# Splitting scores on chip from unit 8 on, and issuing later scores two steps sooner

## The chip, the core and the metric

The kernel runs on one core of one Trainium2 chip. The metric is the device time of one execution in microseconds (us). A core has five engines with a queue each: TensorE (PE, matmuls; its weight loads are listed apart as PEld), VectorE (DVE), ScalarE (ACT), GpSimd (POOL) and SyncE (SP), which here only issues DMAs. Each engine takes its instructions in the order of its queue and waits on semaphores that other engines or DMAs raise.

## The reference

Two stages follow each other. The first is a gated linear recurrence over 4 batches, 8 heads and 768 positions, in chunks; the second a two-layer feed-forward with softplus over the 3072 tokens that come out.

```python
log_a = np.log(np.clip(a, 1e-06, 1.0))
for c in range(nc):                                   # chunks of 32
    cum = np.cumsum(la, axis=-1)
    L = np.exp(cum[:, :, :, None] - cum[:, :, None, :]) * causal
    M = np.einsum('bhin,bhjn->bhij', Cc, Bc) * L      # scores, weighed
    y_intra = np.einsum('bhij,bhjd->bhid', M, xc)
    y_inter = np.einsum('bhin,bhnd->bhid', Cc, state) * decay_to_i[:, :, :, None]
    y[:, :, sl] = y_intra + y_inter
    state = decay_full[:, :, None, None] * state + np.sum(Bx, axis=2)
...
h = x @ w_in                                          # 3072 x 256 @ 256 x 2048
g = np.maximum(h, 0.0) + np.log1p(np.exp(-np.abs(h)))
return (g @ w_out).astype(np.float32)                 # 2048 x 256
```

## The kernel before

**Units.** The recurrence is cut into 24 units of 128 positions, six for each batch; a unit holds all 8 heads. For unit i the names are: `un` its inputs (three buffers in turn), `rm` its decays, `sp_0` and `sp_1` the scores of heads 0-3 and 4-7 in two PSUM banks, `m` the weighed scores, `bp` and `cc` scaled B and C, `zp` the product that updates `state`, `tb` the state spread for reading, `yp_0`, `yp_1` the outputs in PSUM, `y` the grown output, and `xh`, `xl` its high and low part, which the feed-forward reads.

**Two ways to make scores.** The scores of a unit are C times B for 8 heads with 16 rows each, so operands must be laid out with zeros between heads. For units below `FIRST` (12) the host lays them out: `fst` holds, beside x, B and C, a block with the zeros in it, and the kernel multiplies in full fp32, 64 rows to each of the two matmuls (line 386). From unit `FIRST` on, `un` holds B and C stacked plain, 768 KB instead of 576 KB; `split_unit` makes a coarse and a fine row for each on chip: ACT and DVE each pass twice over 128x512 (lines 247 and 248, tiles `c_all` and `b_rows`), two DMAs put `c_all` into the one buffer `c_rows`, whose zeros stay, and four fp32r matmuls of 128x256 make the scores (line 391).

**Feed-forward.** Six token blocks j of 512, 16 feature tiles k each. A pair (j, k) is a first product into a PSUM bank `hp` (six matmuls of 128x512: line 563), softplus to `e` and its high part `gh` on ACT (lines 591, 597), the low part `gl` on DVE (line 603), and a second product of six matmuls into `acc` (line 642). The weights come as 64-bit floats, 512 KB at a time into `wraw`, and are taken apart on ACT and DVE into `wih`, `wil`, `woh`, `wol` (tile `w` on the way; weight step 12 gives `wih` and `wil` for k = 12 and 13). One PSUM pool of six banks serves `hp`, `sp`, `zp`, `yp`; a second holds `acc`.

**What sets the order.** Up to about 86 us the order is the string `ORDER`, written out by hand; everything issued in it stands under line 127 in the profile (the wrapper that keeps program order), and `U7` in it is a step of `update(7)`. After that a loop runs over steps s: `first` and the `e`, `gh`, `gl` of pair s, `second` of pair s-8, and the recurrence's work that `plan` put on step s. A scheduler then orders this part engine by engine. Units 8 to 11 have their scores at steps 20, 22, 25, 28 (`U_STEP`) and their values one step later. Units from 12 on have scores at step 4(i-4) and values two steps after. All DMAs are issued by SP, in program order.

Of the kernel before, what the change touches and what calls it, by code (L numbers as in the profile page):

```python
# [19 lines left out]
NB, NH, S, D, N = 4, 8, 768, 32, 16  # L20
SUB = 32
NC = P // SUB
NU = S // P
# [3 lines left out]
NFT = DFF // P  # L27
TOK = NB * S
HEAD = 4
FIRST = 12  # L30
GU = 3
U_X = 0
U_B = U_X + DM
# [17 lines left out]


ORDER = """
warm1 warm7 la kc hc0 kb un0 w0 loga hc1 loga un1 gb ft0 lr hc2 un2 fr0 ft0 S0 w2 fr0 hc3 D0 fr0 un3 gq0 un4
fr0 w1 D1 W0 gq2 M0 w4 gq0 fr2 M0 S1 gq2 D3 fr2 C1 I0 logr M1 ft2 logr B0 B1 growth U0 C2 U1 U0 W0 fr2
growth T1 B2 fr2 gd U1 ft2 U2 M1 un5 D2 U2 R1 W2 G0 S3 G0 C3 W0 S2 T3 M3 I1 warm3 T2 W0 w6 M2 W0 M3 R3 D4 M2
I3 G1 R2 S4 G1 X0 C4 W0 gg3 I2 warm2 X1 W4 B3 D5 M4 G2 H0 C5 M4 U3 H1 W2 G2 U3 W2 S5 warm4 X2 T4 W2 w3 G3 W2
B4 R4 un6 M5 G3 I4 W2 U4 D6 G4 W1 U4 H2 G4 M5 H3 X3 X4 F0.0 T5 W4 F0.1 W1 P0.0 W4 R5 P0.1 W1 F0.2 P0.0 W4 I5
P0.1 w5 W1 F0.3 W4 D7 w7 G5 S6 warm2 W1 un7 G5 gg6 P0.2 W4 X5 W6 F0.4 M6 P0.2 W6 M6 F0.5 P0.0 W1 P0.3 I6 W6
W3 Z0.0 B6 P0.3 W6 w8 P0.1 U6 W6 U6 C7 Z0.1 W3 W6 P0.4 G6 S7 W5 T7 W3 G6 P0.2 R7 P0.4 F0.6 X6 P0.5 M7 P0.5  # L60
W3 F0.7 w10 M7 W3 P0.3 I7 W3 P0.6 G7 W7 Z0.2 W5 G7 P0.4 X7 P0.7 Z0.3 W5 P0.6 P0.5 W5 P0.7 F1.0 w12 W7 W5
P0.6 F1.1 P1.0 W5 W7 W8 Z0.4 P0.7 P1.1 W7 P1.0 F1.2 w14 W8 B7 W7 W8 W7 Z0.5 P1.2 P1.0 W10 W8 F1.3 P1.1 w9
W10 W8 P1.1 Z0.6 W8 P1.3 W10 W14 F1.4 P1.2 W10 w11 P1.2 W10 Z0.7 W14 P1.4 W10 W14 W9 F1.5 P1.3 W9 W14 F1.6
P1.5 w13 P1.3 W14 W9 F1.7 P1.6 W14 W9 W11 F0.8 w15 W11 W9 W11 F0.9 W9 W11 W13 F0.10 K0 W13 W13 W11 F0.11 W13
W11 W13 Z1.0 W15 W13 W15 W12 U7 Z1.1 W15 P1.4 W12 P1.4 P1.5 Z1.2 W12 P1.7 P1.5 P1.6 W15 Z1.3 P0.9 P1.6 W15
W12 P1.7 Z1.4 U7 W15 P0.11 P1.7 W12 Z1.5 P0.9 W12 P0.10 P0.9 P0.11 Z1.6 P0.8 P0.11 P0.10 Z1.7 P0.10 P0.8 K1
P0.8 zero
"""
HALF = NFT // 2
AHEAD = 20  # L70
# [3 lines left out]
EARLY = 8  # L74
U_STEP = (20, 22, 25, 28)
# [29 lines left out]
def recurrence_then_ffn(ctx: ExitStack, tc: tile.TileContext, fst, un, at, al, w_in, w_out, const, outT):  # L105
# [28 lines left out]
    def load(out, in_):  # L134

        tc.keep_in_program_order(nc.sync.dma_start(out, in_))  # L136

    la = cp.tile([P, NB * NU * NH], F32, name="la")
    lr = cp.tile([P, S * NB * NH // P], F32, name="lr")
    cum = cp.tile([P, S * NB * NH // P], F32, name="cum")  # L140
    kc = cp.tile([P, K_END], F32, name="kc")
    kb = cp.tile([P, C_END], F32, name="kb")
# [6 lines left out]
    gd = dr.tile([NB, NH, S], F32, name="gd")  # L149
# [60 lines left out]
    def load_unit(i):  # L210
# [4 lines left out]
        un_s[i] = p3.tile([P, U_END], F32, tag="un", name=f"un{i}")  # L215
        if i < FIRST:
            load(un_s[i][:, :F_END], fst[i])
        else:
            load(un_s[i], un[i - FIRST])

# [17 lines left out]
    def split_unit(i):  # L238
        if i < FIRST:
            return  # L240
        t = un_s[i]
        b_rows = p2.tile([P, NQ, P], F32R, tag="b_rows", name=f"b_rows{i}")

        def split(out, j):
            raw = t[:, U_S + j * NQ * P : U_S + (j + 1) * NQ * P].rearrange("p (q t) -> p q t", q=NQ)
            g, be = (kb[:, C_GB + v : C_GB + v + 1] for v in (2 * j, 2 * j + 1))
            A.activation(out, raw, AF.Copy, scale=be)
            V.scalar_tensor_tensor(out, raw, g, out.bitcast(F32), op0=ALU.mult, op1=ALU.add)

        c_all = p2.tile([P, NQ, P], F32R, tag="c_all", name=f"c_all{i}")  # L250
        split(c_all, 1)
        for e in range(2):
            rows = slice(64 * e, 64 * e + 64)
            load(c_rows[rows, :, e].bitcast(F32), c_all[rows].bitcast(F32))
        split(b_rows, 0)
        st[i] = b_rows
# [121 lines left out]
    def score(i, g):  # L378
        sp = mid[i]["sp", g] = ps.tile([P, 512], F32, tag="ps", name=f"sp{i}_{g}")
        if i < FIRST:  # L380
            rows = slice(64 * g, 64 * g + 64)
# [292 lines left out]
    def prefetch(i):  # L674
        if i < NB * NU:
            load_unit(i)
            load_growth(i)
# [86 lines left out]
    def plan(s, f, *args):  # L764
        fills[s].append((f, args))

    for i in range(EARLY, NB * NU):
        s, wait = (U_STEP[i - EARLY], 1) if i - EARLY < len(U_STEP) else ((i - HEAD) * NFT // 4, 2)
        plan(s, prepare, i)
        plan(s, attend_scores, i)  # L770
        plan(s + wait, attend_values, i)
        if i + 2 < NB * NU:
            plan(s + 1, prefetch, i + 2)
    for i in range(EARLY, EARLY + 2):
        prefetch(i)
    for s in range(AHEAD, len(steps) + LAG):
        if s < len(steps):
# [56 lines left out]
```

## Time and profile before

| | |
|---|---|
| median of 3 runs (lowest to highest) | 341.74 us (340.98 to 342.81) |
| the profiled execution | 340.56 us, of which the span is 338.8 us |
| PE busy | 328.7 us, 97% of the span |
| DVE, ACT busy | 202.8 us (60%), 171.7 us (51%) |
| HBM read, written | 28.28 MB, 3.24 MB |

The span runs from the first instruction to the last; about 1.8 us of the execution lie around it. Busy times are of one engine; a group of instructions is named by its line, its engine and "output<-input". In the chain that ended last, each piece is followed back to what released it, so its shares add up to the span.

### The profile page before, as it was taken

How to read it: one execution, taken by the hardware profiler on the slowest of the kernel's cores; microseconds unless marked ns; L12 is line 12 of the kernel's file. 1: busy time of each engine (PE TensorE's matmuls, PEld its weight loads, DVE VectorE, ACT ScalarE, POOL GpSimd, SP SyncE). 2: the span in 40 equal slices, each digit the busy share in tenths (PEclk: the TensorE clock that was granted, in tenths of full speed). 3: DMA queues.
4: the chain of work that ended last, by engine and by line, in shares of the span. 5: the costliest groups of instructions: out<-in, count | busy, mean ns of one | idle time of the engine just before them, and what ended most of it. 6: DMA issues, size and time to landing. Idle time of an engine off the chain costs nothing.

```text
span 338.8 us, 5271 instructions
## 1 busy us (share of the span) xinstructions
PE 328.7 (97%) x2047; PEld 249.4 (74%) x2047; DVE 202.8 (60%) x394; ACT 171.7 (51%) x319; POOL 39.3 (12%) x32
## 2 busy tenths in 40 slices
PE   8789998999999999999999999999999999999995
PEld 4446657887666678778778778778778778888885
DVE  0899989996946444864765464777474342232242
ACT  4845666875715435445445455445445244444450
POOL 2434510000111010110112010111010000000000
PEclk9999999999999999999999999999999999999999
DMA  7964533573032205416434205443203100010001
GB/s 233 396 228 138 220 106 104 188 259 120 3 98 114 93 0 189 133 39 186 126 61 141 95 0 188 122 106 99 94 2 93 33 0 0 2 55 8 2 0 62
DMA packets 19376, 35.01 MB, mean 103 GB/s; under 512 B 1432, under 2 KB 10136, under 8 KB 19352
## 3 DMA queue, kind: packets, MB, share of 16 engines
q1 hardware_dynamic: 19352, 34.68, 31.5%
q8 instruction: 16, 0.26, 0.3%
q14 instruction: 8, 0.07, 0.1%
HBM read 28.28 MB, written 3.24 MB: 93 GB/s over the span
## 4 chain that ended last, share of the span: by engine, by line
PE 86%; DVE 6%; DMA 5%; SPq 1%; issue 1%; ACT 0%
PE hp L563 32%; PE acc L642 32%; PE hp L127 6%; PE acc L127 6%; PE yp L466 3%; DMA gg<-gd 3%; DMA head_in_l<-in_fst 2%; PE yp L450 2%; PE sp L391 2%; DVE m L127 1%; DVE w L127 1%; PE sp L386 1%; SPq L136 1%; PE zp L416 1%; PE end L127 1%
## 5 line engine op out<-in xcount | busy, mean ns | idle before, releaser
L603 DVE TENSOR_TENSOR gl<-e,gh 128x512 fp32r<-128x512 f32 x76 | 55.7, 734 | 61.3 <-ACT gh L597 61.1
L597 ACT CAST gh<-e 128x512 fp32r<-128x512 f32 x76 | 47.1, 620 | 61.1 <-PE acc L642 60.3
L591 ACT ACTIVATE e<-hp 128x512 f32<-128x512 f32 x76 | 45.1, 596 | 42.4 <-DVE gl L603 38.5
L563 PE MATMUL hp<-xh,wih 128*128 128x512 f32 x152 | 61.3, 405 | 0.0
L642 PE MATMUL acc<-gl,woh 128*128 128x512 f32 x155 | 60.6, 391 | 0.0
L642 PE MATMUL acc<-gh,wol 128*128 128x512 f32 x155 | 60.5, 391 | 0.0
L642 PE MATMUL acc<-gh,woh 128*128 128x512 f32 x155 | 59.6, 391 | 0.0
L563 PE MATMUL hp<-xl,wih 128*128 128x512 f32 x152 | 59.5, 392 | 0.0
L563 PE MATMUL hp<-xh,wil 128*128 128x512 f32 x152 | 59.3, 391 | 0.0
L345 POOL TENSOR_SCALAR_AFFINE_SELECT rm<-fc 128x1024 f32<-128x1024 f32 x16 | 23.8, 1487 | 187.7 <-DVE m L402 167.8
L563 PEld LDWEIGHTS hp<-xh,wih 128*128 128x128 f32 x152 | 28.5, 188 | 10.7 <-issue 3.1
L642 PEld LDWEIGHTS acc<-gh,woh 128*128 128x128 f32 x155 | 29.1, 188 | 6.8 <-issue 0.8
L642 PEld LDWEIGHTS acc<-gh,wol 128*128 128x128 f32 x155 | 29.1, 188 | 6.2
L642 PEld LDWEIGHTS acc<-gl,woh 128*128 128x128 f32 x155 | 29.1, 188 | 6.1 <-issue 0.2
L563 PEld LDWEIGHTS hp<-xh,wil 128*128 128x128 f32 x152 | 28.5, 188 | 6.3
L563 PEld LDWEIGHTS hp<-xl,wih 128*128 128x128 f32 x152 | 28.6, 188 | 5.1
L402 DVE TENSOR_TENSOR m<-sp,rm 128x512 f32<-128x512 f32 x32 | 20.9, 685 | 7.9 <-PE sp L391 6.3
L127 DVE SCALAR_TENSOR_TENSOR w<-wraw,w 128x512 int32<-128x512 int32 x32 | 23.1, 729 | 0.2
L127 PE MATMUL hp<-xh,wih 128*128 128x512 f32 (+1 forms) x48 | 17.7, 368 | 2.0 <-DVE m L127 1.4
L127 PE MATMUL hp<-xl,wih 128*128 128x512 f32 (+1 forms) x48 | 17.0, 354 | 0.0
L127 PE MATMUL hp<-xh,wil 128*128 128x512 f32 (+1 forms) x48 | 17.0, 354 | 0.0
L127 POOL TENSOR_SCALAR_AFFINE_SELECT rm<-fc 128x1024 f32<-128x1024 f32 x8 | 14.0, 1764 | 20.8 <-DVE m L127 15.0
(109 smaller groups left out, 409.6 us busy)
## 6 DMA issues: line engine op xcount, KB each, us to landing
un<-in_un SPq DMA_DIRECT2D x12, 768.0 KB, 4.4
un<-in_fst SPq DMA_DIRECT2D x8, 576.0 KB, 6.1
wraw<-in_w_in SPq DMA_DIRECT2D x8, 512.0 KB, 3.4
wraw<-in_w_out SPq DMA_DIRECT2D x8, 512.0 KB, 5.2
c_rows<-c_all SPq DMA_DIRECT2D x24, 128.0 KB, 2.4
out_t<-o SPq DMA_DIRECT2D x11, 256.0 KB
gg<-gd SPq DMA_DIRECT2D x14, 192.0 KB
head_in_l<-in_fst SPq DMA_DIRECT2D x4, 320.0 KB, 6.2
```

The costliest lines, as they stand in the source:

```text
L127: return lambda *a, **k: tc.keep_in_program_order(f(*a, **k))
L136: tc.keep_in_program_order(nc.sync.dma_start(out, in_))
L345: Pl.affine_select(out=rm.rearrange("p h c i -> p (h c) i"), in_=fc[:, u].rearrange("p h c -> p (h c)").unsqueeze(2).broadcast_to([P, NH * ...
L391: PE.matmul(sp[:, 2 * v * P : 2 * (v + 1) * P], b_rows[:, q], c_rows[:, q].rearrange("p e t -> p (e t)"), start=True, stop=True,)
L402: V.tensor_tensor(mid[i]["m"][:, 4 * g : 4 * g + 4].rearrange("p h t -> p (h t)"), mid[i].pop(("sp", g)), mid[i]["rm"][:, 4 * g : 4 * g + ...
L450: PE.matmul(yp[q // 2][out], tb[rows].rearrange("p e d -> p (e d)"), cc[rows].rearrange("p c i -> p (c i)"), start=True, stop=False,)
L466: PE.matmul(yp[g][32 * hh : 32 * hh + 32], un_s[i][:, U_X + h * D : U_X + (h + 1) * D], m[:, h, :], start=u == 0, stop=True,)
L563: PE.matmul(h[:, c0:c1], w[:, c, fs], x[:, c, c0:c1], start=i == 0, stop=i == 5)
L591: A.activation(e, h, AF.Softplus)
L597: A.copy(gh, e)
L603: V.tensor_tensor(gl, e, gh.bitcast(F32), op=ALU.subtract)
L642: PE.matmul(acc[:, c0:c1], wo[v, k // HK][:, k % HK, es], g[:, c0:c1], start=start and i == 0, stop=stop and i == 2,)
```

## The change

`FIRST` goes from 12 to 8, so units 8 to 11 are loaded, split and multiplied in the second way. The input of unit 10 is loaded ahead of the loop, with those of 8 and 9, and no longer at step 21. A step of `update(7)`, which reads the buffer that unit 10 takes over, is put earlier in `ORDER` (both `U7` move). From unit 12 on the scores move from step 4(i-4) to 4(i-4)-2, which is the step of the values of the unit in front, and stand behind them; the values stay at their step (wait 4 instead of 2), and the load of unit i+2 moves two steps forward with the scores.

```diff
-FIRST = 12
+FIRST = 8
...
-P1.2 W10 w11 P1.2 W10 Z0.7 W14 P1.4 W10 W14 W9 F1.5 P1.3 W9 W14 F1.6
+P1.2 W10 w11 P1.2 W10 Z0.7 W14 P1.4 W10 W14 W9 U7 F1.5 P1.3 W9 W14 F1.6
...
     for i in range(EARLY, NB * NU):
-        s, wait = (U_STEP[i - EARLY], 1) if i - EARLY < len(U_STEP) else ((i - HEAD) * NFT // 4, 2)
+        s, wait = (U_STEP[i - EARLY], 1) if i - EARLY < len(U_STEP) else ((i - HEAD) * NFT // 4 - 2, 4)
         plan(s, prepare, i)
         plan(s, attend_scores, i)
         plan(s + wait, attend_values, i)
-        if i + 2 < NB * NU:
+        if EARLY + 2 < i + 2 < NB * NU:
             plan(s + 1, prefetch, i + 2)
-    for i in range(EARLY, EARLY + 2):
+    for i in range(EARLY, EARLY + 3):
         prefetch(i)
```

(The lines of `ORDER` are wrapped differently after the change; only `U7` moves in them.) One line fewer stands in `ORDER`, so every line number below it is one lower after the change.

On PE, the scores of unit 8 stand where the hand-written order ends. `acc_1` is the second product of block 1, `hp_12` and `hp_13` first products of block 0. Before:

```order
L127 MATMUL acc_1_944<-gh_7_1003,woh_80 128x512
L563 MATMUL hp_12_1069<-xh_272,wih 128x512
L563 MATMUL hp_12_1069<-xl_273,wih 128x512
L386 MATMUL sp_0_1084<-un_1062 128x512
L386 MATMUL sp_1_1088<-un_1062 128x512
L563 MATMUL hp_13_1095<-xh_272,wih 128x512
```

After:

```order
L126 MATMUL acc_1_951<-gh_7_1005,woh_80 128x512
L562 MATMUL hp_12_1071<-xh_272,wih 128x512
L562 MATMUL hp_12_1071<-xl_273,wih 128x512
L390 MATMUL sp_0_1094<-c_rows,b_rows_1084 128x256 x2
L390 MATMUL sp_1_1099<-c_rows,b_rows_1084 128x256 x2
L562 MATMUL hp_13_1107<-xh_272,wih 128x512
```

The two full-fp32 matmuls give way to four fp32r ones at the same place.

On DVE, the stretch ahead of these matmuls. `un_1138` before and `un_1069` after are the inputs of unit 10, `un_1064` those of unit 9, `w_956` and `w_963` weight step 12, whose next reader is the ACT copy to `wih` for `hp_12`. Before:

```order
L127 TENSOR_TENSOR gl_4_973<-e_4_851,gh_4_970 128x512
L127 SCALAR_TENSOR_TENSOR w_956<-wraw_742,w_956 128x512
L127 TENSOR_TENSOR gl_5_986<-e_5_877,gh_5_975 128x512
L127 SCALAR_TENSOR_TENSOR w_952<-wraw_905,w_952 128x512
L360 TENSOR_TENSOR bp_1258<-un_1138,ft_127 128x128
L376 TENSOR_TENSOR cc_1260<-un_1138,fr_151 128x128
L127 TENSOR_TENSOR gl_6_999<-e_6_892,gh_6_988 128x512
L127 SCALAR_TENSOR_TENSOR w_956<-wraw_742,w_956 128x512
```

After:

```order
L126 TENSOR_TENSOR gl_4_975<-e_4_851,gh_4_972 128x512
L247 SCALAR_TENSOR_TENSOR c_all_1164<-un_1064,kb,c_all_1164 128x512
L247 SCALAR_TENSOR_TENSOR b_rows_1163<-un_1064,kb,b_rows_1163 128x512
L126 SCALAR_TENSOR_TENSOR w_963<-wraw_742,w_963 128x512
L126 TENSOR_TENSOR gl_5_988<-e_5_882,gh_5_977 128x512
L126 SCALAR_TENSOR_TENSOR w_959<-wraw_912,w_959 128x512
L359 TENSOR_TENSOR bp_1288<-un_1069,ft_127 128x128
L375 TENSOR_TENSOR cc_1290<-un_1069,fr_151 128x128
L126 TENSOR_TENSOR gl_6_1001<-e_6_899,gh_6_990 128x512
L247 SCALAR_TENSOR_TENSOR c_all_1270<-un_1069,kb,c_all_1270 128x512
L126 SCALAR_TENSOR_TENSOR w_963<-wraw_742,w_963 128x512
```

Three of the new split instructions are seen here; the two of unit 8 stand a little ahead of the first row, so five in all have come in front of the last one.

On PE, the values of unit 13 and what follows them. Before:

```order
L416 MATMUL zp_1661<-un_1403,bp_1612 32x64 x4
L450 MATMUL yp_0_1668<-cc_1614,tb_1659 64x128 x2
L450 MATMUL yp_1_1669<-cc_1614,tb_1659 64x128 x2
L466 MATMUL yp_0_1668<-m_1606,un_1403 32x128 x4
L466 MATMUL yp_1_1669<-m_1606,un_1403 32x128 x4
L563 MATMUL hp_7_1687<-xh_1134,wih 128x512
```

After:

```order
L449 MATMUL yp_1_1709<-cc_1616,tb_1699 64x128 x2
L465 MATMUL yp_0_1708<-m_1608,un_1443 32x128 x4
L465 MATMUL yp_1_1709<-m_1608,un_1443 32x128 x4
L390 MATMUL sp_0_1737<-c_rows,b_rows_1727 128x256 x2
L641 MATMUL acc_1_1525<-gh_15_1494,woh_855 128x512
L641 MATMUL acc_1_1525<-gl_15_1496,woh_855 128x512
L641 MATMUL acc_1_1525<-gh_15_1494,wol_856 128x512
L641 MATMUL acc_1_1526<-gh_15_1494,woh_855 128x512
L641 MATMUL acc_1_1526<-gl_15_1496,woh_855 128x512
L390 MATMUL sp_1_1742<-c_rows,b_rows_1727 128x256 x2
L641 MATMUL acc_1_1526<-gh_15_1494,wol_856 128x512
L562 MATMUL hp_7_1750<-xh_1146,wih 128x512
```

The scores of unit 14 now follow the values of unit 13 at once, and the next first product comes behind them.

More of the change, by code (lines that the diff above doesn't have):

```diff
@@ L53 @@
 ORDER = """
[L54 to L67, printed above, removed]
+warm1 warm7 la kc hc0 kb un0 w0 loga hc1 loga un1 gb ft0 lr hc2 un2 fr0 ft0 S0 w2 fr0 hc3 D0 fr0 un3 gq0 un4 fr0
+w1 D1 W0 gq2 M0 w4 gq0 fr2 M0 S1 gq2 D3 fr2 C1 I0 logr M1 ft2 logr B0 B1 growth U0 C2 U1 U0 W0 fr2 growth T1 B2
@@ new lines @@
+fr2 gd U1 ft2 U2 M1 un5 D2 U2 R1 W2 G0 S3 G0 C3 W0 S2 T3 M3 I1 warm3 T2 W0 w6 M2 W0 M3 R3 D4 M2 I3 G1 R2 S4 G1
+X0 C4 W0 gg3 I2 warm2 X1 W4 B3 D5 M4 G2 H0 C5 M4 U3 H1 W2 G2 U3 W2 S5 warm4 X2 T4 W2 w3 G3 W2 B4 R4 un6 M5 G3 I4
+W2 U4 D6 G4 W1 U4 H2 G4 M5 H3 X3 X4 F0.0 T5 W4 F0.1 W1 P0.0 W4 R5 P0.1 W1 F0.2 P0.0 W4 I5 P0.1 w5 W1 F0.3 W4 D7
+w7 G5 S6 warm2 W1 un7 G5 gg6 P0.2 W4 X5 W6 F0.4 M6 P0.2 W6 M6 F0.5 P0.0 W1 P0.3 I6 W6 W3 Z0.0 B6 P0.3 W6 w8 P0.1
+U6 W6 U6 C7 Z0.1 W3 W6 P0.4 G6 S7 W5 T7 W3 G6 P0.2 R7 P0.4 F0.6 X6 P0.5 M7 P0.5 W3 F0.7 w10 M7 W3 P0.3 I7 W3
@@ new lines @@
+P0.6 G7 W7 Z0.2 W5 G7 P0.4 X7 P0.7 Z0.3 W5 P0.6 P0.5 W5 P0.7 F1.0 w12 W7 W5 P0.6 F1.1 P1.0 W5 W7 W8 Z0.4 P0.7
+P1.1 W7 P1.0 F1.2 w14 W8 B7 W7 W8 W7 Z0.5 P1.2 P1.0 W10 W8 F1.3 P1.1 w9 W10 W8 P1.1 Z0.6 W8 P1.3 W10 W14 F1.4
+P1.2 W10 w11 P1.2 W10 Z0.7 W14 P1.4 W10 W14 W9 U7 F1.5 P1.3 W9 W14 F1.6 P1.5 w13 P1.3 W14 W9 F1.7 U7 P1.6 W14 W9
+W11 F0.8 w15 W11 W9 W11 F0.9 W9 W11 W13 F0.10 K0 W13 W13 W11 F0.11 W13 W11 W13 Z1.0 W15 W13 W15 W12 Z1.1 W15
+P1.4 W12 P1.4 P1.5 Z1.2 W12 P1.7 P1.5 P1.6 W15 Z1.3 P0.9 P1.6 W15 W12 P1.7 Z1.4 W15 P0.11 P1.7 W12 Z1.5 P0.9 W12
@@ L68 @@
+P0.10 P0.9 P0.11 Z1.6 P0.8 P0.11 P0.10 Z1.7 P0.10 P0.8 K1 P0.8 zero
 """
```

## The prediction, made before the changed kernel was run

> **What bounds the kernel now.** I read the page first, then the list of who waited for whom on PE, then busy time by stage, then the timeline of single engines around 75 to 93 us. The page:
>
> ```profile
> span 338.8 us, 5271 instructions
> PE 328.7 (97%) x2047; PEld 249.4 (74%) x2047; DVE 202.8 (60%) x394; ACT 171.7 (51%) x319; POOL 39.3 (12%) x32
> PE 86%; DVE 6%; DMA 5%; SPq 1%; issue 1%; ACT 0%
> ```
>
> 86% of the chain that ended last is PE itself. Where PE does wait (columns: engine and line, what it waited for, us in total, times, longest), the first and the last of nine rows:
>
> ```profile
> PE hp L127 <- DVE m L127: 1.4, 1, 1.4
> ...
> PE yp L127 <- ACT ft L127: 0.2, 1, 0.2
> ```
>
> They add up to 6.2 us, and all stand under line 127: none is in the scheduled loop. By stage (width, then busy time of PE, PEld, DVE, ACT, POOL with counts, clock, DMA share, GB/s):
>
> ```profile
> 54.00:86.00 32.00, 32.00 (x149) 26.09 (x148) 28.69 (x56) 23.17 (x41) 0.00 (x0) 1.00 0.51 166
> 86.00:134.00 48.00, 48.00 (x296) 33.17 (x295) 27.05 (x54) 22.09 (x40) 5.13 (x4) 1.00 0.26 88
> 134.00:283.00 149.00, 149.00 (x959) 117.28 (x958) 88.32 (x168) 72.00 (x128) 15.44 (x10) 1.00 0.29 86
> ```
>
> From 54 to 283 us PE is never idle and the granted clock is full. So in the whole stretch that the change touches, time goes only if PE gets less to do, and comes only if PE is made to wait. DVE is 90% busy just before (28.69 of 32.00) and 56% after.
>
> **Term 1: cheaper scores.** The two kinds of scores side by side: unit 8 before, and unit 12, which already goes the other way (start, us, line, forms, count):
>
> ```profile
> 86.35 0.39 PE L563 MATMUL hp<-xh,wih 128*128 128x512 f32 x1
> 86.58 0.39 PE L563 MATMUL hp<-xl,wih 128*128 128x512 f32 x1
> 86.90 1.13 PE L386 MATMUL sp<-un 64*128 64x512 f32 x4
> 87.96 0.50 PE L563 MATMUL hp<-xh,wih 128*128 128x512 f32 x1
> 88.29 0.39 PE L563 MATMUL hp<-xl,wih 128*128 128x512 f32 x1
> ...
> 133.61 0.39 PE L642 MATMUL acc<-gh,wol 128*128 128x512 f32 x1
> 133.84 0.64 PE L391 MATMUL sp<-c_rows,b_rows 128*128 128x256 f32 x4
> 134.31 0.40 PE L563 MATMUL hp<-xh,wih 128*128 128x512 f32 x1
> ```
>
> Durations overlap, so I count from start to start. A plain 128x512 matmul takes 0.23 (86.35 to 86.58). With full-fp32 scores it is 1.71 from 86.58 to 88.29 for two plain steps and the scores: 1.71 - 0.45 = 1.26 us, of which 1.06 are the scores and some 0.2 the slow step into them (0.32) and out of them (0.33). With fp32r it is 0.70 - 0.23 = 0.47, and no slow step. Each unit saves 0.79, four units 3.16 us, all on PE. Bounds: both forms are in the trace, so no more than 0.1 either way.
>
> A page bears on this price. The Trainium skill, "FP8 and Floating Point Precision", section Matmul Precision, says that true FP32 takes four passes through the array. My estimate by that page, with the passes of both matmuls one behind the other, would be 8 x 0.23 = 1.84 us for the scores instead of 1.06, and a saving of 6.3 us in all. The row shows 1.06 for both, the 64-row halves running together, so the row decides and the sum does not use the page.
>
> **Term 2: how the full-fp32 groups fall.** The remaining full-fp32 matmuls (zp, yp) also cost a slow step in and out wherever they are put among the others. Counting such groups without the scores in the instruction order, there are 35 before and 36 after: some units' zp and yp come together, others' yp is cut in two. A cut costs 0.09 in, 0.10 out (above) and the end of the last matmul; the shortest group in the trace bounds it:
>
> ```profile
> 108.07 0.39 PE L642 MATMUL acc<-gh,woh 128*128 128x512 f32 x1
> 108.38 0.32 PE L416 MATMUL zp<-un,bp 128*32 128x64 f32 x8
> 108.63 0.50 PE L642 MATMUL acc<-gl,woh 128*128 128x512 f32 x1
> 108.97 0.39 PE L642 MATMUL acc<-gh,wol 128*128 128x512 f32 x1
> ```
>
> 0.90 - 0.45 = 0.45 with its work, so between 0.2 and 0.45; I take +0.3.
>
> **Term 3: a new wait ahead of unit 8.** The splits of units 8 to 10 are now put into the queues of ACT and DVE between 75 and 92 us. DVE there, before (brackets: idle before it, and what ended it), and two splits of unit 12 for their pitch:
>
> ```profile
> 75.63 0.29 DVE L360 TENSOR_TENSOR bp<-un,ft 128x128 f32<-128x128 f32 x1
> 77.03 0.29 DVE L360 TENSOR_TENSOR bp<-un,ft 128x128 f32<-128x128 f32 x1 [0.31 <-DMA un<-in_fst]
> ...
> 83.71 0.29 DVE L360 TENSOR_TENSOR bp<-un,ft 128x128 f32<-128x128 f32 x1 [2.26 <-DMA un<-in_fst]
> 84.12 0.68 DVE L127 TENSOR_TENSOR gl<-e,gh 128x512 fp32r<-128x512 f32 x1
> 84.72 0.68 DVE L127 SCALAR_TENSOR_TENSOR w<-wraw,w 128x512 int32<-128x512 int32 x1
> ...
> 104.49 0.75 DVE L248 SCALAR_TENSOR_TENSOR c_all<-un,kb,c_all 128x512 fp32r<-128x512 f32 x1 [0.46 <-ACT c_all L247]
> 105.16 0.75 DVE L248 SCALAR_TENSOR_TENSOR b_rows<-un,kb,b_rows 128x512 fp32r<-128x512 f32 x1
> ```
>
> Five splits (c_all and b_rows of 8 and 9, c_all of 10) come in front of the `w` at 84.72: 5 x 0.67 = 3.35 us. They fill the idle 0.31 + 2.26 = 2.57, if the inputs of unit 10 are there when DVE asks. That `w` gives `wih` for `hp_12` through ACT:
>
> ```profile
> 80.86 0.62 ACT L127 CAST gh<-e 128x512 fp32r<-128x512 f32 x1 [0.25 <-PE acc L127]
> ...
> 84.83 0.60 ACT L127 ACTIVATE e<-hp 128x512 f32<-128x512 f32 x1 [1.82 <-DVE gl L127]
> 85.44 0.62 ACT L127 CAST wih<-w 128x512 fp32r<-128x512 f32 x1
> ```
>
> `wih` is done at 86.06 and `hp_12` starts at 86.35, so there is 0.29 of slack. The wait is 3.35 - 2.57 - 0.29 = 0.5 us. Behind `hp_12` PE holds everything, so this adds to the time one for one, once; later DVE has 44% idle to catch up. It can't be below 0, since PE has no idle to lose there. The high bound comes from the loads:
>
> ```profile
> 71.07 0.93 SPq L136 DMA_DIRECT2D un<-in_fst  x2
> 72.05 1.12 SPq L136 DMA_DIRECT2D gg<-gd  x2
> 77.94 0.33 SPq L136 DMA_DIRECT2D un<-in_fst  x1
> 134.51 1.27 SPq L136 DMA_DIRECT2D c_rows<-c_all  x2
> ...
> un<-in_un SPq DMA_DIRECT2D x12, 768.0 KB, 4.4
> c_rows<-c_all SPq DMA_DIRECT2D x24, 128.0 KB, 2.4
> ```
>
> The first two blocks, 1.18 MB, went out from 71.07 and had landed by 77.03, where DVE's wait for the second ends: 0.20 MB per us, or 0.33 if the 2.4 us that even a 128 KB copy takes are first set aside. Unit 8's block is 0.2 MB larger and so some 0.6 later; DVE took it at 75.63 without a wait, so 0.6 is the most that this adds. Unit 10's load goes out right behind `gg`, at about 73.2 instead of 77.94, since `U7` is out of its way. Three blocks and `gg` are 2.75 MB: landed by 71.1 + 2.4 + 8.3 = 81.8 at the second rate, 85.0 at the first. I take 81.8, because the fixed part is not paid for each. DVE asks for it at about 83.8; on ACT, c_all, e, woh, gh, e and wih, 0.6 each (84.83 to 85.44), must be done in a row, so ACT asks near 86.35 - 3.6 = 82.7. At the worst rate the wait is 0.5 + 85.0 - 82.7 = 2.8. I take 0.5, the sum of rows.
>
> **What I cost at nothing.** `U7` moved: the same zp on PE, and two DVE instructions of 0.3 at most (as `bp` above) between weights, ahead of 75 us. The copies to `c_rows` for unit 8: c_all is done some 2 us after 75.63, 1.27 for two issues and 2.4 to land end by 82, five us before PE asks. Those for unit 9 wait for unit 8's scores, done near 87.7: plus 1.27 and 2.4 is 91.4, while PE comes to them 25 plain steps, four score steps and one zp-yp group (about 1.5) after `hp_12` begins: 86.85 + 5.7 + 0.5 + 1.5 = 94.5. They now stand in SP's queue ahead of the load of unit 11, which waits for unit 8's yp (near 92.7) in any case; it lands 4.4 later at 97.1, and unit 9's second `m`, which stands behind unit 11's `cc` and a `gl` on DVE, is done 1.4 after that, at 98.5. PE needs it near 99.8 (16 plain steps, scores and most of a zp-yp group further). Had that load the 5.8 of unit 10's (77.94 to 83.71), it would be just in time. The splits of units 9 to 11 behind that are 1.3 us a unit on DVE and on ACT, under PE. Scores two steps sooner for units 12 to 23: PE does the same matmuls and waited for none of them, so nothing is to be had; DVE, ACT and SP merely change order.
>
> **Sum.** -3.16 + 0.3 + 0.5 = -2.4 us. The profiled execution took 340.56 (338.8 and 1.8 around it), 1.2 below the median shown, so it would become 338.2; against the median, 341.74 - 2.4 = 339.4 us, 0.7% less.
>
> **Rivals.** (a) The early wait eats the gain. For it: DVE is 90% busy up to 86 us, and one late load holds up everything behind it. The row at 83.71 shows that: `gl` at 84.12 had its input since `gh` ended near 81.5 and stood behind `bp`. The Trainium skill, "TensorE: Matmul & The Clock Gate", in its section on the array's architecture, says that ACT and DVE queues are strict FIFO; the trace agrees. If ACT's c_all of unit 10 is held by the load, every us past 82.7 is a us of PE; at 1.2 of wait (landing at 83.4) the change is under 0.5% (1.7 us, about what a measurement of this kernel can tell from no change), at 2.9 (85.1) it is nil: 341.7. Against it: 0.9 us between the landing I take and ACT's need. (b) The other side: PSUM banks. The scores of the next unit now come straight behind yp, so zp, two yp and two sp hold five of six banks when `hp` wants one, 0.24 + 1.13 + 0.24 + 0.23 = 1.84 us after yp ends. Had that to be the bank of the second `m`, free at about 2.5 (sp begins at 1.6, about 0.3 to its end, 0.6 for `m`, taken as a `gl`), PE would wait 0.65 on each of 12 units: 7.8 us, 347 us. It makes the kernel slower by 0.5% from 0.34 us a unit. Against it: zp's and yp's banks fall free earlier:
>
> ```profile
> 138.96 0.65 PE L466 MATMUL yp<-m,un 128*32 128x128 f32 x16
> 139.53 0.50 PE L563 MATMUL hp<-xh,wih 128*128 128x512 f32 x1
> ...
> 140.18 0.48 DVE L477 TENSOR_TENSOR y<-yp,gg 128x128 f32<-128x128 f32 x2
> ```
>
> `y` ends 1.1 us after yp here, 0.7 ahead of that. (c) Slightly more gain: no early wait and no cut, 338.6 or below.
>
> **How the numbers follow.** Forecast 0.58 (338.6 to 340.0), (c) 0.07, (a) 0.22 (340.0 to 343.4), (b) 0.13. Faster 0.65, same 0.22, slower 0.13. The range goes from 337.9, (c) with the scatter of a median, to 341.7, where (a) has eaten all; it leaves out (b) and the top of (a).
>
> **What would show it.** Four more units with line 390 matmuls 0.47 apart and no 64-row ones; a PE pause of about 0.5 before `hp_12` near 86.4, ended by ACT; no DVE wait for unit 10's load of 2 us; PE without idle from there to 283. It is wrong if PE waits again and again in the loop, or if unit 10 lands after 83.4.

## The result, and the profile after

The changed kernel is slower. Its median is 345.74 us (343.88 to 347.51, 4 runs) against 341.88 (340.98 to 342.81, 4 runs) for the kernel before on the same chip: ratio 1.0125, interval 1.0086 to 1.0164. The forecast was 339.4, the range 337.9 to 341.7. The profiled execution of the changed kernel took 345.08 us, 4.5 more than that of before. Ratios, here and below, are the record's over fast runs and not quotients of the medians; one run of e3 and one of e6 were slow and stand in those two medians alone.

The page after the change. The first row of engines answers to that of before; below it the clock that TensorE was granted, a digit for each fortieth of the span, and the chain that ended last by engine:

```profile
span 343.3 us, 5296 instructions
PE 330.2 (96%) x2047; PEld 251.6 (73%) x2047; DVE 208.7 (61%) x402; ACT 176.0 (51%) x327; POOL 38.6 (11%) x32
PEclk9899989999999999999999999999999999999999
PE 82%; DMA 7%; DVE 6%; ACT 2%; issue 1%; POOL 1%; SPq 1%; ACTq 0%; DVEq 0%; POOLq 0%
```

PE's share of the chain fell from 86% to 82% and that of DMA rose from 5% to 7%. The clock has two dips, in the second and sixth slice (9 to 17 and 43 to 51 us), both in the head; looked at closely they are two stretches at half clock, 14.42 to 17.83 and 48.55 to 51.96 us (granted clock 0.50 in each). By stage, in the same columns as in the prediction:

```profile
54.00:86.00 32.00, 32.00 (x151) 26.09 (x147) 30.57 (x61) 24.41 (x42) 0.00 (x0) 1.00 0.59 190
86.00:134.00 48.00, 44.99 (x292) 33.03 (x291) 34.38 (x63) 24.29 (x44) 7.79 (x5) 1.00 0.37 107
134.00:283.00 149.00, 149.00 (x953) 116.31 (x952) 84.89 (x165) 72.13 (x127) 12.00 (x9) 1.00 0.30 88
```

PE now stands still for 3.01 us of the 48 behind 86 us, where it had no idle before. PE's timeline there (in brackets the idle time ahead of a matmul, and what ended it):

```profile
87.80 0.39 PE L126 MATMUL acc<-gh,woh 128*128 128x512 f32 x1
90.06 0.50 PE L126 MATMUL acc<-gl,woh 128*128 128x512 f32 x1 [1.87 <-DVE gl L126]
...
91.94 0.51 PE L126 MATMUL acc<-gh,woh 128*128 128x512 f32 x1 [0.47 <-ACT gh L126]
92.95 0.50 PE L562 MATMUL hp<-xh,wih 128*128 128x512 f32 x1 [0.50 <-ACT wih L126]
93.29 0.40 PE L562 MATMUL hp<-xl,wih 128*128 128x512 f32 x1
93.52 0.63 PE L390 MATMUL sp<-c_rows,b_rows 128*128 128x256 f32 x4
93.99 0.40 PE L562 MATMUL hp<-xh,wih 128*128 128x512 f32 x1
```

From start to start, and less the 0.23 of a plain step, the three waits take 2.03, 0.62 and 0.78 us; a fourth at 86.54 takes 0.34. That is 3.8 us ahead of the scores of unit 8, where the prediction had 0.5. The scores themselves are as cheap as forecast: 0.70 from 93.29 to 93.99 for a plain step and the scores.

The chain of work that ended last, in order of time, tells whose wait it was (start, us, what):

```profile
80.77 0.69 SPq L135
...
81.50 8.05 DMA c_rows<-c_all
...
89.66 0.10 ACT c_all L246
...
90.29 0.58 ACT e L126
90.87 0.51 ACT woh L126
91.37 0.45 ACT gh L126
...
92.28 0.62 ACT wih L126
...
92.95 0.73 PE hp L562 x2
```

A copy of unit 8's `c_all` into `c_rows` took 8.05 us, where the median of these copies before was 2.4. What waits for it is not PE's scores but ACT, which wants to write the `c_all` of unit 10. Tiles `c_all` have two buffers, so unit 10 takes that of unit 8, and may do so only when the copies have read it. On ACT and DVE:

```profile
89.66 0.72 ACT L246 ACTIVATE c_all<-un,kb 128x512 fp32r<-128x512 f32 x1 [4.56 <-DMA c_rows<-c_all]
```
```profile
88.91 0.29 DVE L359 TENSOR_TENSOR bp<-un,ft 128x128 f32<-128x128 f32 x1 [1.82 <-DMA un<-in_un]
89.32 0.68 DVE L126 TENSOR_TENSOR gl<-e,gh 128x512 fp32r<-128x512 f32 x1
```

ACT stood for 4.56 us; `e`, `woh`, `gh` and `wih` queued behind. DVE stood for 1.82 for the load of unit 10, with the `gl` behind it that PE wanted at 88. Both transfers were late. SP's queue:

```profile
74.13 0.93 SPq L135 DMA_DIRECT2D un<-in_un  x2
75.11 1.26 SPq L135 DMA_DIRECT2D gg<-gd  x2
76.42 1.12 SPq L135 DMA_DIRECT2D un<-in_un  x1
80.77 14.70 SPq L135 DMA_DIRECT2D c_rows<-c_all  x4
```

The last row counts the copies of units 8 and 9 together; those of unit 8 are issued by 82.1.

The growth factors `gg` of unit 9 (two loads of 192 KB) go out just ahead of the load of unit 10. The load, issued from 76.42 on, is taken by DVE at 88.91: some 12 us later, where the one of 576 KB before took 5.8 (77.94 to 83.71). While all wait, the DMA engines are mostly idle (the last two columns are their busy share and GB/s):

```profile
78.00:84.00 6.00, 6.00 (x28) 4.95 (x27) 5.69 (x14) 5.35 (x10) 0.00 (x0) 1.00 1.03 313
84.00:90.00 6.00, 4.01 (x17) 2.67 (x15) 4.18 (x8) 1.44 (x3) 0.00 (x0) 1.00 0.23 72
```

A share of 0.23 and 72 GB/s, after 1.03 and 313 in the six us ahead: 0.23 of 16 is 3.7, so what is left would run on about four of the sixteen engines. The Trainium skill, "DMA: Bandwidth & Descriptors", section "Queues, rings and completion order", says that one copy is split over up to 16 rings, not always all, and that each DMA engine consumes the descriptors of a ring in order. That fits: a small copy issued behind a transfer that fills a few rings is complete only when its parts in those rings have had their turn. The packets in the trace of after show it. Their size tells whose they are: 1536 bytes are rows of `gg`, 6144 of `un`, 512 of `c_rows`. The 256 packets of `gg` run from 80.2 to 86.2 us, 3.9 at a time in the mean. Of the 512 packets of unit 8's copies 384 have landed by 84.4; the last 128, a quarter, start only at 87.5 and end at 89.0, behind the last packets of unit 10's load (to 87.6). So a quarter of each transfer waits behind `gg`. In e2 below, where `gg` goes last, all 512 have landed by 84.0. The experiments with the place of `gg` test what this costs.

### The profile page after: what moved, and what is told of

The parts are those of the page before. It is cut to its first block, busy times and chain, and to the rows that moved or that the text cites. A ratio compares the mean times of both kernels' runs of the same rounds, so it can differ in the third digit from the quotient of the medians.

```text
span 343.3 us, 5296 instructions
## 1 busy us (share of the span) xinstructions
PE 330.2 (96%) x2047; PEld 251.6 (73%) x2047; DVE 208.7 (61%) x402; ACT 176.0 (51%) x327; POOL 38.6 (11%) x32
## 4 chain that ended last, share of the span: by engine, by line
PE 82%; DMA 7%; DVE 6%; ACT 2%; issue 1%; POOL 1%; SPq 1%; ACTq 0%; DVEq 0%; POOLq 0%
PE acc L641 31%; PE hp L562 31%; PE hp L126 4%; DMA gg<-gd 3%; PE acc L126 3%; PE yp L465 3%; PE sp L390 3%; DMA c_rows<-c_all 2%; PE yp L449 2%; DVE m L126 2%; DVE w L126 1%; DMA un<-in_un 1%; PE warm L126 1%; PE zp L415 1%; PE sp L126 1%
## 5 line engine op out<-in xcount | busy, mean ns | idle before, releaser
L602 DVE TENSOR_TENSOR gl<-e,gh 128x512 fp32r<-128x512 f32 x76 | 57.0, 754 | 66.5 <-ACT gh L596 66.5
L641 PE MATMUL acc<-gh,woh 128*128 128x512 f32 x155 | 60.7, 395 | 0.0
L562 PE MATMUL hp<-xh,wih 128*128 128x512 f32 x152 | 59.8, 394 | 0.5 <-ACT wih L126 0.5
L344 POOL TENSOR_SCALAR_AFFINE_SELECT rm<-fc 128x1024 f32<-128x1024 f32 x16 | 23.0, 1438 | 186.4 <-DVE m L401 173.9
L246 ACT ACTIVATE c_all<-un,kb 128x512 fp32r<-128x512 f32 x16 | 11.6, 723 | 26.7 <-DMA un<-in_un 22.0
L359 DVE TENSOR_TENSOR bp<-un,ft 128x128 f32<-128x128 f32 x13 | 5.7, 437 | 22.2 <-DMA un<-in_un 22.1
```

Source lines behind the costliest of these rows:

```text
L344: Pl.affine_select(out=rm.rearrange("p h c i -> p (h c) i"), in_=fc[:, u].rearrange("p h c -> p (h c)").unsqueeze(2).broadcast_to([P, NH * ...
L562: PE.matmul(h[:, c0:c1], w[:, c, fs], x[:, c, c0:c1], start=i == 0, stop=i == 5)
L602: V.tensor_tensor(gl, e, gh.bitcast(F32), op=ALU.subtract)
L641: PE.matmul(acc[:, c0:c1], wo[v, k // HK][:, k % HK, es], g[:, c0:c1], start=start and i == 0, stop=stop and i == 2,)
```

## The experiments

Theory: `gg` of unit 9, ahead of the load of unit 10 and of unit 8's copies, delays both; the copies hold ACT through the two buffers of `c_all`, the load holds DVE, and PE waits. Rivals: the five splits in front of `w` cost this by themselves (so the order of the DMAs doesn't matter); the sooner scores do it, in the loop; the new layout of the inputs in HBM does it.

Since executions scatter by some us, I read each profile in stages as well, between the 200th, 325th and 950th matmul of `hp` and `acc` on PE (the 48 half-width `hp` of the head are counted with the plain ones of 128x512). The stages hold the same work in every kernel, apart from the edits: up to 200 is the hand-written head, 200 to 325 holds the wait and units 8 to 11, 325 to 950 the loop. Times are in us, worked out from the start times of these matmuls.

| kernel | median, runs | ratio to before (interval) | to 200 | 200-325 | 325-950 |
|---|---|---|---|---|---|
| before | | 1 | 78.38 | 38.93 | 166.32 |
| after | 345.74, 4 | 1.0125 (1.0086 to 1.0164) | 80.98 | 40.04 | 167.14 |
| e1 before again | 342.04, 12 | 1.0007 (0.9982 to 1.0032) | 78.47 | 38.91 | 166.32 |
| e2 `gg` later | 341.49, 12 | 0.9998 (0.9971 to 1.0025) | 81.21 | 37.21 | 167.14 |
| e3 split from 8 alone | 344.58, 12 | 1.0059 (1.0025 to 1.0093) | 79.38 | 40.79 | 166.29 |
| e4 sooner alone | 343.46, 12 | 1.0055 (1.0028 to 1.0081) | 81.04 | 38.93 | 168.14 |
| e5 after again | 345.83, 4 | 1.0123 (1.0089 to 1.0157) | 79.92 | 39.70 | 167.21 |
| e6 `gg` later, not sooner | 340.81, 12 | 0.9978 (0.9947 to 1.0009) | 80.41 | 37.20 | 166.29 |
| e7 inputs laid out anew | 342.37, 10 | 1.0034 (1.0004 to 1.0064) | 82.15 | 38.92 | 166.31 |
| e8 `gg` between | 345.18, 2 | 1.0114 (1.0075 to 1.0152) | 81.08 | 40.56 | 167.13 |
| e9 after, not sooner | 344.75, 12 | 1.0071 (1.0040 to 1.0102) | 79.69 | 40.36 | 166.29 |
| e10 = e2 again | 340.96, 12 | 0.9969 (0.9939 to 0.9999) | 78.16 | 37.17 | 167.19 |
| e11 = e6 again | 340.57, 12 | 0.9961 (0.9933 to 0.9989) | 80.01 | 37.10 | 166.29 |

e1 to e4, e5 to e8 and e9 to e11 ran on one chip each, with their own runs of the kernel before (medians 341.53, 341.00, 341.81).

The 4.5 us between the two profiled executions are 2.60 in the head, 1.11 in the stage of the wait and 0.82 in the loop. The 2.60 are not waiting: PE is idle for 6.46 us of the head before and 6.44 after. Its busy time there is longer by as much (71.92 and 74.54), for the same matmuls, and the two stretches at half clock lie in it. In the 1.11 the wait of 3.8 us and the cheaper scores (about 2.7, see below) meet.

**e1: the kernel before, unchanged.** No edit; it shows what no change looks like.

> The kernel before, once more, to see by the granted clock of its own runs whether the first 54 us vary by themselves. Theory (loads in SP's queue, chance at the start): its runs scatter by 1 to 2 us and some show a mean clock under 1.0 (0.99), as the runs after the change do. Rival (the change itself slows the start): all runs keep 1.00 and lie within 1 us.

Measured: 1.0007, the middle stages within 0.02 us of the first profile. Its runs lie 2.3 us apart (340.65 to 342.95), with mean clocks from 0.994 to 1.000; the 0.983 to 0.990 of three of the four runs after don't occur. Further repeats agree within 0.1 us past the head (e2 and e10, e6 and e11), after and e5 within 0.34 in the stage of the wait; what goes well beyond that is an effect.

**e2: `gg` of unit 9 behind unit 8's copies.** The changed kernel, with one edit:

```diff
     for i in range(EARLY, EARLY + 3):
-        prefetch(i)
+        load_unit(i)
+    plan(AHEAD, load_growth, EARLY + 1)
```

> The kernel after, with the load of gg for units 9 to 11 taken from ahead of unit 10's load to behind the copies of unit 8's c_all. Theory (gg's small rows fill a few DMA rings, and unit 10's load and unit 8's copies wait behind them): unit 10 lands 5 us or more sooner, c_all of unit 10 on ACT no longer waits 4.6 us, the PE pauses between 86 and 93 us go from 3.8 to under 1 us, and the time falls by 2.5 to 3.5 us against the kernel after, to about the time before or 1 us below. Rival (the five splits themselves overfill DVE and ACT ahead of unit 8): the pauses stay at 3 us or more and the time within 1 us of the kernel after.

Measured: 0.9998, the whole loss gone, and 2.8 us less in the stage 200-325 than after. On ACT the wait shrinks from 4.56 to 0.42, and SP's queue shows the new order:

```profile
84.43 0.72 ACT L246 ACTIVATE c_all<-un,kb 128x512 fp32r<-128x512 f32 x1 [0.42 <-DMA c_rows<-c_all]
```
```profile
74.36 1.41 SPq L135 DMA_DIRECT2D un<-in_un  x3
81.12 1.37 SPq L135 DMA_DIRECT2D c_rows<-c_all  x2
82.54 1.16 SPq L135 DMA_DIRECT2D gg<-gd  x2
```

All splits are still in front of `w`, and PE's waits ahead of unit 8 fall from 3.8 to 1.04, so the rival of the splits falls: it was the order of the transfers.

**e3: the split from unit 8 alone.** The kernel before, with

```diff
-FIRST = 12
+FIRST = 8
```

so that `U7`, unit 10's load and the loop stay as they were.

> Only the split from unit 8 on: no early load of unit 10, U7 at its old place, no scores sooner. Theory (the early load of unit 10 and what is queued with it made the pause, the cheaper scores are real): 1.5 to 3 us below the kernel before, unless unit 8's copies behind gg hold PE up (then about the time before). Rival (splits overfill the queues): slower than before by 1 us or more.

Measured: 1.0059, and 40.79 in the stage 200-325, the slowdown that the rival had forecast. The rows name another cause: unit 10's load goes out late (issued at 80.21) and ACT waits for that, and PE through `gh`:

```profile
87.49 0.72 ACT L247 ACTIVATE c_all<-un,kb 128x512 fp32r<-128x512 f32 x1 [4.59 <-DMA un<-in_un]
```
```profile
89.77 0.66 PE L127 MATMUL acc<-gh,woh 128*128 128x512 f32 x1 [2.50 <-ACT gh L127]
```

The split alone runs into a wait of the same size from another transfer. Moving the load forward, as the change does, gained little while `gg` stood ahead of it: e9 below, which is this kernel with the early load and the moved `U7`, has 1.0071. Whether the early load is needed once `gg` is behind was not run.

**e4: sooner scores alone.** The kernel before, with

```diff
-... else ((i - HEAD) * NFT // 4, 2)
+... else ((i - HEAD) * NFT // 4 - 2, 4)
```

> Only the scores two steps sooner from unit 12 on; units 8 to 11 as before. Theory (PE waited for none of these scores): within 0.7 us of the kernel before, with the same start. Rival (banks or queues in the loop give PE new waits): 1 us or more slower, with PE idle between 134 and 283 us.

Measured: 1.0055, the loop 1.82 us longer, the stage before it unchanged. One wait of 0.64 and 0.17 us is seen in it,

```profile
141.03 0.43 PE L466 MATMUL yp<-m,un 128*32 128x128 f32 x8 [0.64 <-ACT e L591]
141.63 0.50 PE L391 MATMUL sp<-c_rows,b_rows 128*128 128x256 f32 x2 [0.17 <-ACT e L591]
```

which is not there in the changed kernel. ACT's `e` is read by neither `yp` nor `sp`; what it frees is the PSUM bank of the `hp` that it has read, so this looks like rival (b) on a small scale. The rest is in how the full-fp32 matmuls are cut, below at e9 to e11. The groups of full-fp32 matmuls in this loop are the same 18 as in the changed kernel, against 17 before. The sooner scores cost time in the loop; I had put them at nothing.

**e5: the changed kernel again.** No edit, on the chip of e6 to e8.

> The kernel after, once more, on the chip and beside the runs of e6 to e8. Theory (most of the loss is the PE pause between 86 and 93 us, the start varies by chance): the pauses at unit 8 add up to 3 to 4 us again in a new profile, the start (to 60 us) differs from the first profile's by up to 2 us; time 3 to 4.5 us above the kernel before. Rival (a bad draw of the start): 2 us above or less.

Measured: 1.0123 against 1.0125 the first time. PE stands for 2.7 us in the stage of the wait (1.61, 0.57 and 0.50 us), 3.0 the first time.

**e6: `gg` later, and the scores at their old steps.** The edit of e2, and that of e4 taken back.

> As e2 (gg behind the copies), and the scores from unit 12 on at their old step. Theory (the split is worth 2.5 to 3 us on PE, the early splits cost about 1, scores sooner cost 0.7 in the loop by cut-up groups of full-fp32 matmuls): 0.7 us below e2, so 0.7 to 2 us below the kernel before. Rival (scores sooner cost nothing in this setting): as e2, within 0.3 us.

Measured: 0.9978 (0.9947 to 1.0009), the loop back at 166.29. This leaves the cheaper scores, the early load and `gg` in its new place.

**e7: the layout alone.** The kernel before, with its inputs cut in HBM as after the change: `fst` for 8 units, `un` for 16, and the full-fp32 blocks of units 8 to 11, which this kernel still uses, in an input of their own (`fsu`). Of the edit, the line that loads a unit:

```diff
-            load(un_s[i][:, :F_END], fst[i])
+            load(un_s[i][:, :F_END], fst[i] if i < EARLY else fsu[i - EARLY])
```

> The kernel before with the same instructions, but its inputs cut as after: the host-made blocks of units 0 to 7 in one tensor, of units 8 to 11 in another at the end, and the plain tensor holding 16 units. Theory (the later landing of gg near 46 us in all three kernels that split from unit 8 on comes from where the inputs lie in HBM): PE's wait for tb near 46 us is 1.4 us or more instead of 0.7, and the time 0.5 to 1.5 us above the kernel before. Rival (chance): 0.7 us of wait and the time within 0.5 us of the kernel before.

Measured: 1.0034 (1.0004 to 1.0064), with the stages past the head as before. It can't have made the 1.2%; whether it makes 0.3% in the head is open. In its profile the head is 3.8 us longer than before, but PE is idle there for 6.01 us, not more than the 6.46 before: the matmuls of the first 14 us take about twice as long (four `sp` 2.08 us at 7.67, where they take 1.13 before). Late loads are not what made this head long.

**e8: `gg` behind unit 10's load, still ahead of the copies.** The changed kernel, with

```diff
     for i in range(EARLY, EARLY + 3):
-        prefetch(i)
+        load_unit(i)
+    load_growth(EARLY + 1)
```

> The kernel after, with gg for units 9 to 11 loaded behind unit 10's block, but still ahead of the copies of unit 8's c_all. Theory (ACT's c_all of unit 10 takes the buffer of unit 8's and so waits for those copies, which wait behind gg in the rings): unit 10 lands 4 us or more sooner, the copies still take 6 to 8 us, and PE's pauses near 86 to 93 us stay at 2 us or more. Rival (it was unit 10's own load alone): pauses under 1.2 us, as in e2.

Measured: 1.0114 from two runs, as slow as after, although DVE no longer waits for the load. ACT still waits for the copies:

```profile
75.68 1.10 SPq L135 DMA_DIRECT2D gg<-gd  x2
80.86 14.59 SPq L135 DMA_DIRECT2D c_rows<-c_all  x4
```
```profile
88.78 0.73 ACT L246 ACTIVATE c_all<-un,kb 128x512 fp32r<-128x512 f32 x1 [3.78 <-DMA c_rows<-c_all]
```

PE stands for 0.39, 1.43 and 0.50 us ahead of unit 8, 2.3 in all where it was 3.0 after. So the copies behind `gg` and the buffer of `c_all` are enough for a wait of nearly the same size; the late load stood beside it. The 40.56 of this profile's stage also holds a stretch at half clock (see below), so it doesn't size the wait.

**e9 to e11, on one chip: sooner or not, `gg` before or behind.** e9 is the changed kernel with the old steps of the scores; e10 is e2 and e11 is e6, each again.

> The changed kernel with the scores from unit 12 on back at their old steps; gg and the copies as in the change. If the sooner scores cost the 0.85 us that the two profiles with gg later showed in the loop: 345.0 us, 1.010 of before, with the long pause ahead of unit 8 kept. If they cost nothing and all of the loss is the pause and what follows it: 345.8, 1.0125 of before.

> gg of unit 9 behind the copies, sooner scores kept; the same kernel as before in this study, now on one chip with the next. 341.5 us, 1.000 of before; PE 0.85 us longer than the next kernel between 100 and 283 us.

> gg of unit 9 behind the copies, old steps. If the sooner scores cost 0.85 us: 0.0025 below the kernel beside it, so 340.6 us, 0.9975 of before, and the interval of ten more runs tells whether this version beats the kernel before. If the sooner scores cost nothing, as the prediction said: 341.5, 1.000.

Measured: 344.75, 340.96 and 340.57. e9 and e11 differ in the place of `gg` alone: 4.2 us. Of these 3.3 are seen in the profiles' stage 200-325 (40.36 and 37.10), in e9 with a stretch at half clock. After and e5, with none in that stage, are 2.5 to 2.9 above e2 and e10. e10 and e11 differ in the sooner scores alone: 0.90 us in the loop; in the medians 0.4, which two medians with this scatter don't tell from 0.9. e11 beats the kernel before by 0.4% (interval 0.9933 to 0.9989) and its ratio is 1.6% below that of after. It has the lowest ratio, though e10's 0.9969 can't be told from it; e6, the same kernel, had 0.2% with an interval that reaches 1.0009, so its gain over before is some 1 us.

Where the 0.90 us are is seen on PE. In the kernel after (and in e10) the values of unit 23 are cut through the middle of `yp`:

```profile
267.68 0.32 PE L415 MATMUL zp<-un,bp 128*32 128x64 f32 x8
267.93 0.43 PE L449 MATMUL yp<-cc,tb 32*64 32x128 f32 x4
268.29 0.42 PE L465 MATMUL yp<-m,un 128*32 128x128 f32 x8
268.65 0.50 PE L641 MATMUL acc<-gh,woh 128*128 128x512 f32 x1
...
269.31 0.43 PE L449 MATMUL yp<-cc,tb 32*64 32x128 f32 x4
269.68 0.43 PE L465 MATMUL yp<-m,un 128*32 128x128 f32 x8
270.03 0.50 PE L390 MATMUL sp<-c_rows,b_rows 128*128 128x256 f32 x2
```

In e11 the same values run in one piece:

```profile
266.06 0.32 PE L415 MATMUL zp<-un,bp 128*32 128x64 f32 x8
266.31 0.45 PE L449 MATMUL yp<-cc,tb 32*64 32x128 f32 x8
266.69 0.64 PE L465 MATMUL yp<-m,un 128*32 128x128 f32 x16
267.26 0.50 PE L562 MATMUL hp<-xh,wih 128*128 128x512 f32 x1
```

The whole piece takes 1.20 us (266.06 to 267.26). Cut, the halves take 0.97 (267.68 to 268.65) and 0.72 (269.31 to 270.03), 1.69 together, and a second slow step out. The second half costs 0.2 inside one piece and 0.7 as a piece of its own: four `yp` from `cc` take 0.36, as long as eight (0.38), and eight from `m` take 0.36 against 0.57 for sixteen. Unit 15 is cut in the same way. By start times, the full-fp32 groups of the loop take 15.44 us in after and 14.46 in e11, which is 0.98 more, twice the 0.49 of one such cut. The other steps nearly cancel: scores 0.83 more, plain steps 0.97 less, since 8 of the 18 groups are now followed by scores, on which the slow step out of a group then falls.

**The clock.** The lost time in medians is more than the idle time of PE in some profiles. The granted clock of PE in the 6 us behind the wait, in e3 and e8:

```profile
90.00:96.00 6.00, 5.66 (x21) 4.43 (x21) 5.30 (x8) 4.36 (x9) 1.67 (x1) 0.72 0.24 48
```
```profile
90.00:96.00 6.00, 4.43 (x14) 3.50 (x15) 5.52 (x10) 5.26 (x10) 0.76 (x1) 0.72 0.09 18
```

The mean is 0.72 here, 0.80 in e9, and 1.00 in the profiles of after, e5, e2, e6, e10 and e11. It is the mean of two speeds. Taken alone, 89.94 to 93.36 us of e3, 91.83 to 95.25 of e8 and 88.97 to 92.38 of e9 each have a granted clock of 0.50: one stretch of 3.4 us at half clock, and 1.00 around it. In e3 the plain step behind the scores of unit 8 takes 0.42 (92.65 to 93.07), in after 0.23. My estimate from this: such a stretch costs up to 1.7 us, half of its length, where PE is busy. So a wait of this size is followed by half clock in some executions and not in others. The mean granted clock over all runs fits: 0.989 to 0.994 for after, e3, e5, e8 and e9, which have the long wait, and 0.996 to 0.998 for e1, e2, e4, e6, e7, e10 and e11, which have not. That the place of `gg` changes it is shown (0.9908 in e9, 0.9971 in e11); that the wait itself sets it off is argued, since the two stretches of after lie in the head. The difference of 0.0063, times 342 us, is 2.2: by this estimate up to half of the 4.2 us between e9 and e11 is slower clock, and the rest PE standing still (2.06 us in e9, 0.58 in e11). The Trainium skill, "TensorE: Matmul & The Clock Gate", in its table of clock states, gives an idle window of about 3.4 us as what brings the cold state; the longest idle piece of PE in the 3.4 us ahead of the stretch is 2.50 us in e3, 1.86 in e9 and 1.43 in e8, so on this the runs show a dip from less. Pieces of 1.87 in after and 1.61 in e5 brought none.

## Why the prediction was wrong, point by point

- **Term 1, cheaper scores (-3.16), right.** The scores of unit 8 in e10:

```profile
87.59 0.40 PE L562 MATMUL hp<-xl,wih 128*128 128x512 f32 x1
87.83 0.63 PE L390 MATMUL sp<-c_rows,b_rows 128*128 128x256 f32 x4
88.29 0.40 PE L562 MATMUL hp<-xh,wih 128*128 128x512 f32 x1
88.53 0.39 PE L562 MATMUL hp<-xl,wih 128*128 128x512 f32 x1
```

Two plain steps with scores take 0.94 (87.59 to 88.53); before it was 1.71. That is 0.77 a unit where I had 0.79.

- **Term 2, cuts (+0.3), right up to the loop.** e11's stage 200-325 is 1.83 below that of before and holds 0.9 of waits (0.55 and 0.36), so the scores and cuts together gave -2.7; I had -2.86. For the loop I counted groups, one more, and priced each cut alike; a cut through the middle of `yp` costs about 0.5 (1.69 against 1.20), above the bound of 0.45 that I took from a `zp` alone.
- **Term 3, the wait ahead of unit 8 (+0.5): this is the step that failed.** I took 81.8 for the landing of unit 10's load, with 85.0 as the worst. DVE took it at 88.91, in an execution whose head was 2.6 us later, so at 86.3 by the prediction's clock, past the bound. The working added up bytes and divided by a rate, so `gg` counted as 0.39 MB at 0.33 MB per us, 1.2 us. Its packets took 6.0 us after (80.2 to 86.2), and 5.4 already in the trace of before (76.4 to 81.8), where 77 to 79 us show a DMA share of 0.30 and 83 GB/s against 0.98 and 380 from 72 to 76. `gg` and what stands behind it leave most DMA engines idle; bytes over rate is no bound for a transfer that queues behind such a load.
- **"The copies to `c_rows` for unit 8 ... end by 82, five us before PE asks": wrong twice.** They took 8.05 us, not 2.4, for the same reason; and the one who asks first is not PE but ACT, for the buffer of `c_all`, at 85.1 (89.66 less 4.56). I never asked who writes that buffer next. e8 shows that this alone is enough.
- **Five splits on DVE.** With the transfers out of the way (e2, e10, e11) the waits that remain ahead of unit 8 are 0.9 to 1.05 us; the 0.5 that I worked out was half of it.
- **"Scores two steps sooner ... nothing to be had": wrong by 0.9 us**, through the cuts.
- **Rivals.** (a), the early wait that eats the gain, is what came, with the copies to `c_rows`, which it didn't name, beside the late load, and at a size beyond the 343.4 where I let it end; the range stopped at 341.7. (b), PSUM banks in the loop, did not: PE is busy 149.00 of 149.00 us from 134 to 283, with no wait; only e4 has one of 0.81 in all.

The sum in place of mine, from the runs: -2.7 for scores and cuts, 0.9 for the splits' waits, 4.2 for `gg` ahead of the copies (e9 against e11, with the clock in it), 0.9 for the sooner scores: +3.3 us. Measured were 3.9 and 4.8 (345.74 - 341.88, 345.83 - 341.00). About 1 us stays open. The head is where a single profile strays most: one and the same kernel reached the 200th matmul at 81.21 in e2 and at 78.16 in e10, and a median of four doesn't average that out. The traces say what strays there: e2 has a stretch at half clock from 16.07 to 19.49 us and 0.8 us more of idle PE, e10 has no such stretch. Why an execution has one in the head is not shown. Near 46 us PE's wait for `tb` of unit 3 was 2.0 after against 0.7 before, though the change leaves that place alone; it was 1.4 in e3 and e5, 1.5 in e2, 1.35 in e8, 1.2 to 1.5 in e9 to e11, 0.7 in e6, 0.8 in e4 and 0.9 in e7. Neither the layout nor chance is shown to be its cause; PE's idle time in the head as a whole is the same before and after. A third buffer for `c_all`, which would part the copies from ACT, wasn't run.

## What to carry to other kernels

When a change adds a small transfer, look at what stands ahead of it in the issuing queue and on how many DMA engines that runs: a few hundred KB on a few engines can hold a 128 KB copy for 8 us, while the DMA share reads 23%. Ask of each new tile not only who reads it but who writes its buffer next; with two buffers, a late reader stops the writer two units on, and everything behind it on that engine's queue. Where a matmul group of another kind is put, what counts is where it is cut: two halves of `yp` took 1.69 us where the whole took 1.20. And when two profiles differ by a few us, look first whether PE waited longer or only ran slower: here 2.6 of 4.5 us lay in a stretch where it waited no longer.

## What the runs showed of the hardware that I had not expected

- A copy of 128 KB between SBUF tiles landed after 8.05 us behind two loads of 192 KB, and after 2.4 in the median of the kernel before; the DMA engines were 23% busy meanwhile, and the last quarter of the packets of unit 8's two copies started 3 us after the rest had landed.
- Pauses of PE of 1.4 to 2.5 us were followed by 3.4 us at half clock in three profiles (e3, e8, e9), and by none in two others (after, e5).
- Halves of a full-fp32 group cost much more than half: 0.97 and 0.72 us where the whole took 1.20.
